# Attention and a routed feed-forward: routing choices in one pass, spaced key and value rows

## The chip, the cores and the metric

The kernel runs on one core of a Trainium2 chip. The metric is the time of one execution on the device in microseconds, lower is better. One execution was also taken by the hardware profiler; its rows are quoted below. TensorE appears as PE, its weight loads as PEld, VectorE as DVE, ScalarE as ACT, GpSimd as POOL and SyncE as SP.

## The reference

Masked attention over 8 batches of 8 heads, sequence 576 and head width 64, whose output is the input of a mixture of experts over 4608 tokens of width 512. Every token takes the best of 4 groups and in it the best of 4 experts, and its output is that expert's feed-forward (hidden width 1024) weighed by both softmax weights.

```python
mask_plain = (rel >= 0) & (rel < 32)
mask_dil = (rel >= 0) & (rel < 128) & (rel % 4 == 0)
# heads 0-3 plain, heads 4-7 dilated
scores = np.where(masks[None], scale * q @ k.T, -1e9)
attn = softmax(scores); x = (attn @ v) -> (4608, 512)
g_idx = np.argmax(x @ w_group, axis=1); g_w = softmax(...)[g_idx]
e_idx = np.argmax(x @ w_expert[g_idx], axis=1); e_w = softmax(...)[e_idx]
out = (g_w * e_w)[:, None] * (np.maximum(x @ w1[g, e], 0) @ w2[g, e])
```

## The kernel before

**Attention.** The batches are taken in four pairs (NBP), each in nine tiles (NJ) of 64 positions, 36 tiles (NT). One tile covers all 16 sequences of the pair. The loop `for s in range(NT + 3)` is pipelined by hand: step s issues scores of tile s, the transposition of the probabilities of tile s-1 (transpose_p), the product with the values of tile s-2 (av, into the accumulator o, of which there is one), its normalisation on VectorE, and the transposition of the normalised x of tile s-3 (transpose_x). On VectorE a tile has the row maximum mx, d = s - mx, the sums den, their reciprocal, and x = o * den. The orders of TensorE and VectorE are those of the code; the two queues are not sorted again. Since o has one buffer, the next av can begin only when x has read it.

**Loads.** q, k and v come in by groups of three tiles (192 positions), SP's queue issues all loads and stores in order. load_k fills every other partition of kb with a row of 8 * 224 numbers (7,168 bytes) per half; load_v fills vt with three blocks of 8 * 65 numbers per partition, in pieces of two and one (4,160 and 2,080 bytes a row, 6,240 where all three go at once). GpSimd makes a shifted copy of v (shift_v).

**Routing.** When the nine tiles of a pair are through, route(bp) follows, a Python generator that issues the routing of its 1152 tokens (TPB = 9 blocks of 128) in steps: the logits by TensorE (lt_ps, lg_ps), the choice of the group and then of the expert in it (top1, called twice), the one-hot matrix E, the ranks of the tokens within their expert by matmuls (rk_ps), the slot of each token, its split in a high part and 7 low bits (hl), the gate gt (written to the token's row in DRAM), and two masks, ohl (which of 128 low values) and mv (which high value, times the token's number). Their product tb_ps over nine blocks of tokens is the table of tokens by slot (tab). `yield` ends a step; a step that ends in `yield 2` closes the gate until the next av has been issued. slot() is called five times per tile, between VectorE's five instructions of attention, and runs fine[0] steps of the routing in hand. pick(r) chooses the expert with most tokens so far, for an early FFN, after the routings of two and of three pairs. The routings of the first three pairs run beside attention, the fourth in the tail.

**Tail.** After the last tile a string, TAIL, says in which order the rest is issued: R a part of the last route up to a gate, a and b a step of the first and second early FFN, w a chunk of weights. A chunk is split into two 16-bit parts: wb1h and the like on ScalarE, the rest wb1l on VectorE, which needs the first. After that come the 16 experts' FFNs, three matmuls per product (high times high, high times low, low times high).

Of the kernel before, what the change touches and what calls it, by code (L numbers as in the profile page):

```python
# [17 lines left out]
P = 128  # L18
# [27 lines left out]
TAIL = "aRaRaRawawwawRaRbwaRwbbwbbbwbwbw"  # L46
# [9 lines left out]
def moe_attention_kernel(ctx, tc, q, k, k0, v, cmask, wgate, wpack, out):  # L56
# [34 lines left out]
    KW = 8 * 224 + 96  # L91
# [67 lines left out]
    nc.gpsimd.iota(low, pattern=[[1, P]], base=0, channel_multiplier=0, allow_small_or_imprecise_dtypes=True)  # L159
    iota = low[:, 0:MAXOV]  # L160
# [19 lines left out]
    mine1 = cp.tile([P, TPB], F32, name="mine1")  # L180
# [4 lines left out]
    high = cp.tile([P, NE, NK4], F32, name="high")  # L185
# [29 lines left out]
    routes, gate, fine = [], [], [SLOTS]  # L215
# [7 lines left out]
    def scores(n):  # L223
# [144 lines left out]
    def route(bp):  # L368
# [24 lines left out]

        def top1(l4, nm):
            mx = T("mx" + nm, [TPB])
            nc.vector.tensor_reduce(mx, l4, axis=AX.X, op=ALU.max)
            yield 0
            mb = mx.unsqueeze(2).broadcast_to([P, TPB, 4])
            oh = T("oh" + nm, [TPB, 4])
            nc.vector.tensor_tensor(oh, l4, mb, ALU.is_equal)  # L400
            yield 0
            nc.vector.tensor_tensor(oh, oh, pri.unsqueeze(1).broadcast_to([P, TPB, 4]), ALU.mult)
            yield 0
            pm = T("pm" + nm, [TPB])
            nc.vector.tensor_reduce(pm, oh, axis=AX.X, op=ALU.max)
            yield 0
            nc.vector.tensor_tensor(oh, oh, pm.unsqueeze(2).broadcast_to([P, TPB, 4]), ALU.is_equal)
            df = T("df" + nm, [TPB, 4])
            nc.vector.tensor_tensor(df, l4, mb, ALU.subtract)
            yield 0  # L410
            return oh, df

        def total(df, nm):
            s = T("sm" + nm, [TPB])
            nc.vector.tensor_reduce(s, df, axis=AX.X, op=ALU.add)
            yield 0
            nc.vector.tensor_scalar_add(s, s, 1e-9)
            return s

        ohg, dfg = yield from top1(lg[:, :, 0:4], "g")  # L420
        yield 1
        pr = T("pr", [TPB, 4, 4])
        nc.vector.tensor_tensor(
            pr,
            lg[:, :, 4:20].rearrange("p t (g e) -> p t g e", g=4),
            ohg.unsqueeze(3).broadcast_to([P, TPB, 4, 4]),
            ALU.mult,
        )
        yield 0
        el = T("el", [TPB, 4])  # L430
        nc.vector.tensor_reduce(el, pr.rearrange("p t g e -> p t e g"), axis=AX.X, op=ALU.add)
        yield 0
        ohe, dfe = yield from top1(el, "e")
        E = E16[bp % 2]
        nc.vector.tensor_tensor(
            E[:, 0:TPB],
            ohg.unsqueeze(3).broadcast_to([P, TPB, 4, 4]),
            ohe.unsqueeze(2).broadcast_to([P, TPB, 4, 4]),
            ALU.mult,
        )  # L440
        yield 2
# [11 lines left out]
        for df in (dfg, dfe):  # L453
            nc.scalar.activation(df, df, AF.Exp, scale=1.0 / SX)
# [4 lines left out]
        nc.vector.tensor_copy(base[bp + 1], rk[:, TPB, :])  # L459
        nc.vector.tensor_tensor(rk[:, 0:TPB], rk[:, 0:TPB], Ef[:, 0:TPB], ALU.mult)  # L460
        yield 0
        mine = slice(bp * TPB, bp * TPB + TPB)
        nc.vector.tensor_reduce(slots[:, mine], rk[:, 0:TPB], axis=AX.X, op=ALU.add)
        yield 0
        sli = T("sli", [2, TPB], I32)
        nc.vector.tensor_copy(sli[:, 0], slots[:, mine])
        nc.vector.tensor_single_scalar(sli[:, 1], sli[:, 0], 7, ALU.arith_shift_right)
        yield 0
        hl = T("hl", [2, TPB])
        nc.vector.tensor_copy(hl[:, 1], sli[:, 1])  # L470
        nc.vector.scalar_tensor_tensor(hl[:, 0], hl[:, 1], -float(P), slots[:, mine], ALU.mult, ALU.add)
        yield 0
        sg = yield from total(dfg, "g")
        se = yield from total(dfe, "e")
        yield 0
        nc.vector.tensor_tensor(sg, sg, se, ALU.mult)
# [3 lines left out]
        own = xd[bp * TPB * P : (bp + 1) * TPB * P, DM:XW]  # L480
        nc.sync.dma_start(own.rearrange("(t p) o -> p t o", p=P), gt)
        tb_ps = psR.tile([P, NE * NK4], F32, name="tb_ps", tag="r")
        done = []
        for t0 in range(0, TPB, 3):
            ohl = sm.tile([P, 3, P], F16, name="ohl", bufs=2)
            nc.vector.tensor_tensor(
                ohl,
                low.unsqueeze(1).broadcast_to([P, 3, P]),
                hl[:, 0, t0 : t0 + 3].unsqueeze(2).broadcast_to([P, 3, P]),
                ALU.is_equal,  # L490
            )
            yield 0
            mv = sm.tile([P, 3, NE * NK4], F16, name="mv", bufs=2)
            for t in range(3):
                nc.vector.tensor_scalar(
                    mv[:, t],
                    high.rearrange("p e k -> p (e k)"),
# [672 lines left out]
```

## Time and profile before

| what | value |
|---|---|
| time, median of 3 runs | 610.18 us (608.88 to 617.73) |
| the profiled execution | 610.33 us |
| its span in the trace | 608.4 us |
| TensorE busy | 549.1 us, 90% |
| VectorE busy | 395.0 us, 65% |
| ScalarE, GpSimd busy | 316.8 and 206.1 us |
| instruction fetches | 63 of 1.03 MB in all (queue q8) |

The span is the time from the first to the last record of the trace; the profiled execution's own time holds 1.9 us more around it. Three stretches are told apart by their place in the program: attention with three routings up to about 185 us, the tail up to about 212 us, and the experts after that. A wait is the idle time of an engine ahead of an instruction, with what released it. "issue" means that nothing in the trace ended the wait. The granted clock is a share of TensorE's full speed.

### The profile page before, as it was taken

The page shows a single profiled execution, that of the slowest core. Times are in us where ns is not written, and L with a number is a line of the kernel's source. Part 1 is how long each engine was busy: PE and PEld are TensorE (multiplying, and loading weights), DVE is VectorE, ACT ScalarE, POOL GpSimd, SP SyncE. Part 2 cuts the span into 40 slices and gives each one's busy share as a digit, 9 for nine tenths or more (in the row PEclk, how much of TensorE's full clock was granted, in tenths as well). Part 3 has the DMA queues.
Part 4 walks back from the last instruction along what each step waited for, and adds up shares of the span by engine and source line. Part 5 has one row for each costly group of instructions (what it writes and reads, how often), then busy time and mean ns, then how long its engine had stood idle before and what let it go on. Part 6 is the DMA issues. An engine that isn't in the chain of part 4 may idle for free. (4 is left out here: it accounts for less than half of the span.)

```text
span 608.4 us, 18962 instructions
## 1 busy us (share of the span) xinstructions
PE 549.1 (90%) x7796; PEld 387.0 (64%) x7796; DVE 395.0 (65%) x923; ACT 316.8 (52%) x558; POOL 206.1 (34%) x243
## 2 busy tenths in 40 slices
PE   4787978879868599999999999999999999999985
PEld 2565756657556366656665666756657657787773
DVE  4465696796996772285577759767376577567730
ACT  3454434544564242374454647556486567566641
POOL 5886454544202022532033161322623502221211
PEclk9999989999989599999999999999999999999988
DMA  8988679777757416286959788696877989898840
GB/s 321 363 256 275 185 215 281 212 221 242 235 154 231 142 48 208 61 224 214 257 172 297 208 252 219 204 305 201 270 180 264 300 236 298 284 307 238 242 118 29
DMA packets 82764, 136.44 MB, mean 224 GB/s; under 512 B 43149, under 2 KB 52791, under 8 KB 82675
## 3 DMA queue, kind: packets, MB, share of 16 engines
q1 hardware_dynamic: 75746, 115.62, 63.4%
q0 software_dynamic: 6784, 19.51, 10.3%
q8 instruction: 63, 1.03, 0.7%
q14 instruction: 27, 0.21, 0.1%
q10 hardware_dynamic: 144, 0.07, 0.0%
HBM read 108.12 MB, written 19.29 MB: 209 GB/s over the span
## 5 line engine op out<-in xcount | busy, mean ns | idle before, releaser
L696 DVE SCALAR_TENSOR_TENSOR hl<-a,hh 128x256 f16<-128x256 f32 (+13 forms) x144 | 60.3, 423 | 83.5 <-ACT hh L695 67.8
L752 POOL DMA_INDIRECT out<-yr,sent x31 | 38.4, 1240 | 216.5 <-ACT yr L751 194.1
L688 PE MATMUL a<-xs,wb1h 128*128 128x256 f16 (+7 forms) x576 | 99.8, 279 | 0.9 <-ACT xs L664 0.5
L688 PE MATMUL a<-xs,wa1h 128*128 128x304 f16 (+7 forms) x576 | 96.3, 274 | 1.4 <-SPq L1081 0.9
L695 ACT ACTIVATE hh<-a 128x256 f16<-128x256 f32 (+13 forms) x144 | 55.7, 389 | 71.0 <-PE a L688 57.4
L781 PEld LDWEIGHTS <-hh 128*128 128x128 f16 x480 | 46.9, 98 | 54.6 <-issue 1.2
L688 PE MATMUL a<-xs,wb1l 128*128 128x256 f16 (+7 forms) x288 | 79.3, 279 | 0.6 <-DVE wb1l L603 0.6
L688 PE MATMUL a<-xs,wa1l 128*128 128x304 f16 (+7 forms) x288 | 77.5, 274 | 0.1
L688 PEld LDWEIGHTS <-wb1h 128*128 128x128 f16 x576 | 55.9, 99 | 13.3 <-issue 0.6
L688 PEld LDWEIGHTS <-wa1h 128*128 128x128 f16 x576 | 55.2, 99 | 13.0 <-issue 2.0
L631 POOL DMA_INDIRECT xr<-xd,sent x41 | 42.1, 1027 | 45.4 <-DVE key L560 23.1
L117 POOL TENSOR_SCALAR vs<-vt 32x520 f32<-32x520 f32 (+1 forms) x48 | 41.1, 856 | 46.0 <-DMA vt<-v 38.4
L603 DVE SCALAR_TENSOR_TENSOR wa2l<-w,wa2h 128x1024 f16<-128x1024 f32 x32 | 38.6, 1219 | 26.7 <-ACT wa2h L606 24.5
L603 DVE SCALAR_TENSOR_TENSOR wb2l<-w,wb2h 128x1024 f16<-128x1024 f32 x32 | 38.8, 1222 | 21.4 <-ACT wb2h L606 19.2
L279 PE MATMUL o<-vs,pt 64*32 64x65 f32 x1152 | 34.1, 232 | 17.8 <-DVE x L335 12.3
L781 PE MATMUL y<-wa2h,hh 128*128 128x512 f16 x120 | 45.6, 380 | 0.5 <-issue 0.5
L781 PE MATMUL y<-wb2h,hl 128*128 128x512 f16 x120 | 45.5, 379 | 0.5 <-DVE hl L696 0.5
L781 PE MATMUL y<-wb2h,hh 128*128 128x512 f16 x120 | 45.6, 380 | 0.0
L781 PE MATMUL y<-wb2l,hh 128*128 128x512 f16 x120 | 45.5, 379 | 0.0
L781 PE MATMUL y<-wa2l,hh 128*128 128x512 f16 x120 | 45.5, 379 | 0.0
L781 PE MATMUL y<-wa2h,hl 128*128 128x512 f16 x120 | 45.5, 379 | 0.0
L253 DVE TENSOR_REDUCE mx<-s 128x8 f32<-128x512 f32 x36 | 24.7, 687 | 30.8 <-PE s L243 30.8
(199 smaller groups left out, 1210.5 us busy)
## 6 DMA issues: line engine op xcount, KB each, us to landing
w<-wpack SPq DMA_DIRECT2D x128, 512.0 KB
kb<-k SPq DMA_DIRECT2D x24, 448.0 KB
qb<-q SPq DMA_DIRECT2D x28, 256.0 KB
vt<-v SPq DMA_DIRECT2D x11, 520.0 KB
xd<-x SPq DMA_DIRECT2D x24, 192.0 KB
vt<-v SPq DMA_DIRECT2D x11, 260.0 KB
qb<-q SPq DMA_DIRECT2D x2, 768.0 KB
xd<-x SPq DMA_DIRECT2D x32, 48.0 KB
```

The costliest lines, as they stand in the source:

```text
L117: nc.gpsimd.tensor_scalar(vs[g][even, j0:j1], vt[g][even, j0:j1], 1.0, 1.0, ALU.mult, ALU.mult)
L253: nc.vector.tensor_reduce(mx, s, axis=AX.X, op=ALU.max)
L279: nc.tensor.matmul(o[32 * j : 32 * j + 32, w, c * 65 : c * 65 + 65], pt[n % NPT][64 * w : 64 * w + 64, c, 32 * j : 32 * j + 32], (vs, vt)[ ...
L603: nc.vector.scalar_tensor_tensor(l, w32, SW, h, ALU.mult, ALU.subtract)
L631: nc.gpsimd.indirect_dma_start(out=xr[0:n], out_offset=None, in_=xd[0:known, :], in_offset=bass.IndirectOffsetOnAxis(ap=ent[0:n, t : t + 1 ...
L688: nc.tensor.matmul(a[:, 0:cap], ww[:, c * FF + f * P : c * FF + f * P + P], xx[:, c, 0:cap], start=(i == 0), stop=(i == len(mm) - 1),)
L695: nc.scalar.activation(hh[:, f, 0:cap], a[:, 0:cap], AF.Relu)
L696: nc.vector.scalar_tensor_tensor(hl[:, f, 0:cap], a[:, 0:cap], 0.0, hh[:, f, 0:cap], ALU.max, ALU.subtract)
L752: ins = nc.gpsimd.indirect_dma_start(out=out, out_offset=bass.IndirectOffsetOnAxis(ap=ent[0:n, t : t + 1], axis=0), in_=yr[0:n, :], in_off ...
L781: nc.tensor.matmul(yp, h[:, f, t * P : t * P + n], ww[:, f * DM : f * DM + DM], start=(i == 0), stop=(i == len(mm) - 1),)
```

## The change

It has three parts. **Routing:** the maxima, one-hots and differences of the group and of all four groups' experts are taken at once, over 5 * 9 rows of four, and E is one product of both; exponential on 180 elements. The sums, the gate's reciprocal (now on 9 elements) and the update of base follow after the product tb_ps, and the gate is spread to 16 columns by ScalarE. The masks mv are two instructions over 128x576 in 16 bit, ohl three of 128x384 with a 16-bit index row; the nine tb_ps matmuls stand together after one gate. fine[0], the number of steps per slot, is 1 until the third routing starts and 2 (SLOTS) from there on; it was 2 throughout. **Loads:** the four parts of a k row lie 456 numbers apart in kb and the three blocks of a v row 528 numbers apart in vt, so that one row is moved in pieces of 1,792 or 2,080 bytes. **Tail:** the string is another.

```diff
-TAIL = "aRaRaRawawwawRaRbwaRwbbwbbbwbwbw"
+TAIL = "aRaRawawawRwawbwabRwabbwbbbwbw"
-    KW = 8 * 224 + 96
+    KC = 448 + 8
+    KW = 4 * KC + 96
         for w in halves:
-            nc.sync.dma_start(kb[g % NK][w:P:2, w, 0 : 8 * 224], k[g, w])
+            nc.sync.dma_start(
+                kb[g % NK][w:P:2, w, 0 : 4 * KC].rearrange("p (c n) -> p c n", n=KC)[:, :, 0:448],
+                k[g, w].rearrange("p (c n) -> p c n", n=448),
+            )
-            vt[g] = vp.tile([P, 3, 8, 65], F32, name="vt")
+            vt[g] = vp.tile([P, 3, 528], F32, name="vt")[:, :, 0:520].rearrange("p j (s c) -> p j s c", c=65)
-    high = cp.tile([P, NE, NK4], F32, name="high")
+    high = cp.tile([P, NE, NK4], F16, name="high")
-    routes, gate, fine = [], [], [SLOTS]
+    routes, gate, fine = [], [], [1]
-                    c0 = sl * w + 32 * (jl + a)
+                    c0 = sl * w + 32 * (jl + a) + (8 * (sl // 2) if n else 0)
...
-        ohg, dfg = yield from top1(lg[:, :, 0:4], "g")
-        yield 1
...
-        ohe, dfe = yield from top1(el, "e")
+        n5 = 5 * TPB
+        l5 = lg.rearrange("p t (g e) -> p (t g) e", e=4)
+        mx = T("mx5", [n5])
+        nc.vector.tensor_reduce(mx, l5, axis=AX.X, op=ALU.max)
+        yield 0
+        mb = mx.unsqueeze(2).broadcast_to([P, n5, 4])
+        oh = T("oh5", [n5, 4])
+        nc.vector.tensor_tensor(oh, l5, mb, ALU.is_equal)
...
+        ohv = oh.rearrange("p (t g) e -> p t g e", g=5)
+        ohg = ohv[:, :, 0, :]
         E = E16[bp % 2]
         nc.vector.tensor_tensor(
-            E[:, 0:TPB],
-            ohg.unsqueeze(3).broadcast_to([P, TPB, 4, 4]),
-            ohe.unsqueeze(2).broadcast_to([P, TPB, 4, 4]),
-            ALU.mult,
+            E[:, 0:TPB], ohg.unsqueeze(3).broadcast_to([P, TPB, 4, 4]), ohv[:, :, 1:5, :], ALU.mult
         )
...
-        gt = T("gt", [TPB, XW - DM])
-        nc.vector.reciprocal(gt, sg.unsqueeze(2).broadcast_to([P, TPB, XW - DM]))
...
+        mv = T("mv", [TPB, NE * NK4], F16)
+        nc.vector.tensor_tensor(
+            mv,
+            high.rearrange("p e k -> p (e k)").unsqueeze(1).broadcast_to([P, TPB, NE * NK4]),
+            hl[:, 1].unsqueeze(2).broadcast_to([P, TPB, NE * NK4]),
+            ALU.is_equal,
+        )
+        yield 0
+        nc.vector.tensor_tensor(mv, mv, mine1.unsqueeze(2).broadcast_to([P, TPB, NE * NK4]), ALU.mult)
+        yield 0
+        ohl = T("ohl", [TPB, P], F16)
         for t0 in range(0, TPB, 3):
-            ohl = sm.tile([P, 3, P], F16, name="ohl", bufs=2)
...
-            for t in range(3):
-                nc.vector.tensor_scalar(
-                    mv[:, t],
...
+        yield 2
+        tb_ps = psR.tile([P, NE * NK4], F32, name="tb_ps", tag="r")
+        for t in range(TPB):
+            nc.tensor.matmul(tb_ps, ohl[:, t], mv[:, t], start=(t == 0), stop=(t == TPB - 1))
+        s5 = T("s5", [n5])
+        nc.vector.tensor_reduce(s5, df, axis=AX.X, op=ALU.add)
...
+        nc.vector.reciprocal(sg, sg)
+        gt = T("gt", [TPB, XW - DM])
+        nc.scalar.copy(gt, sg.unsqueeze(2).broadcast_to([P, TPB, XW - DM]))
...
+        nc.vector.tensor_copy(base[bp + 1], rk[:, TPB, :])
         yield 1
...
-            if n == NBP - 3:
+            if n == NBP - 2:
                 fine[0] = SLOTS
```

VectorE's row before, in the tile of the first routing that makes the masks: mx, d, den, the reciprocal of den and x are attention's, all else is the routing's.

```order
L255 TENSOR_TENSOR d<-s,mx 128x512
L417 TENSOR_SCALAR sme<-sme 128x9
L476 TENSOR_TENSOR smg<-smg,sme 128x9
L328 TENSOR_SCALAR den<-o 128x8
L479 RECIPROCAL gt<-smg 128x144
L486 TENSOR_TENSOR ohl<-low,hl 128x384
L495 TENSOR_SCALAR mv<-high,hl,mine_204 128x64 x3
L330 RECIPROCAL den<-den 128x8
L486 TENSOR_TENSOR ohl<-low,hl 128x384
L495 TENSOR_SCALAR mv<-high,hl,mine_204 128x64 x3
L335 TENSOR_TENSOR x<-o,den 128x2x4x64
L253 TENSOR_REDUCE mx<-s 128x8
```

VectorE's row in the changed kernel, in the tile of the first routing that makes the masks (high and low_174 are index rows, hl the split slots).

```order
L259 TENSOR_REDUCE mx<-s 128x8
L457 TENSOR_TENSOR mv<-high,hl 128x576
L261 TENSOR_TENSOR d<-s,mx 128x512
L464 TENSOR_TENSOR mv<-mv,mine_206 128x576
L334 TENSOR_SCALAR den<-o 128x8
L468 TENSOR_TENSOR ohl<-low_174,hl 128x384
L336 RECIPROCAL den<-den 128x8
L468 TENSOR_TENSOR ohl<-low_174,hl 128x384
L341 TENSOR_TENSOR x<-o,den 128x2x4x64
L468 TENSOR_TENSOR ohl<-low_174,hl 128x384
L259 TENSOR_REDUCE mx<-s 128x8
```

Between den and x there stand two ohl in place of gt, two ohl and six mv; the masks mv are made between mx and den, and the gate's sums have left this place.

VectorE's row before, in the tail, from the early FFN's hl to the split of the last routing's slots; wb1l are the low halves of the second early expert's weights.

```order
L696 SCALAR_TENSOR_TENSOR hl<-a,hh 128x128 x2
L603 SCALAR_TENSOR_TENSOR wb1l<-w_3925,wb1h 128x1024
L603 SCALAR_TENSOR_TENSOR wb1l<-w_3927,wb1h 128x1024
L457 TENSOR_TENSOR rk<-rk_ps,base_150 128x160
L459 COPY base_151<-rk 128x16
L460 TENSOR_TENSOR rk<-rk,E_199 128x144
L463 TENSOR_REDUCE slots<-rk 128x9
L466 CAST sli<-slots 128x9
L467 TENSOR_SCALAR sli<-sli 128x9
L470 CAST hl<-sli 128x9
L471 SCALAR_TENSOR_TENSOR hl<-hl,slots 128x9
```

VectorE's row in the changed kernel at the same place of the tail.

```order
L686 SCALAR_TENSOR_TENSOR hl<-a,hh 128x128 x3
L593 SCALAR_TENSOR_TENSOR wb1l<-w_3829,wb1h 128x1024
L438 TENSOR_TENSOR rk<-rk_ps,base_150 128x160
L441 TENSOR_TENSOR rks<-rk,E_201 128x144
L444 TENSOR_REDUCE slots<-rks 128x9
L447 CAST sli<-slots 128x9
L449 TENSOR_SCALAR sli<-sli 128x9
L452 CAST hl<-sli 128x9
L454 SCALAR_TENSOR_TENSOR hl<-hl,slots 128x9
L457 TENSOR_TENSOR mv<-high,hl 128x576
L464 TENSOR_TENSOR mv<-mv,mine_206 128x576
L468 TENSOR_TENSOR ohl<-low_174,hl 128x384 x3
L593 SCALAR_TENSOR_TENSOR wb1l<-w_3831,wb1h 128x1024
L593 SCALAR_TENSOR_TENSOR wb1l<-w_3833,wb1h 128x1024
```

One split of weights stands ahead of rk where there were two, no gate sum follows the split of the slots, and two more splits come after the masks.

ScalarE's row before, in the tail, at the high halves wb1h of the second early expert's weights; xs is the second early FFN's input, yr an output of the first.

```order
L606 ACTIVATE wb1h<-w_3925 128x1024
L606 ACTIVATE wb1h<-w_3927 128x1024
L606 ACTIVATE wb1h<-w_3929 128x1024
L454 ACTIVATE dfg<-dfg 128x36
L454 ACTIVATE dfe<-dfe 128x36
L751 ACTIVATE yr<-y,cse_223 128x512
L664 CAST xs<-pt 128x4x128 x2
L606 ACTIVATE wb1h<-w_3931 128x1024
L606 ACTIVATE wb2h<-w_3950 128x1024
```

ScalarE's row in the changed kernel at the same place.

```order
L596 ACTIVATE wb1h<-w_3829 128x1024
L685 ACTIVATE hh<-a 128x128
L596 ACTIVATE wb1h<-w_3831 128x1024
L435 ACTIVATE df_3812<-df_3812 128x180
L596 ACTIVATE wb1h<-w_3833 128x1024
L596 ACTIVATE wb1h<-w_3835 128x1024
L654 CAST xs<-pt 128x4x128 x2
L596 ACTIVATE wb2h<-w_3869 128x1024
```

The fourth wb1h stands ahead of the casts of xs, and no yr stands ahead of them.

## Rows read from the trace of the kernel before

**Rows 1.** Windows: stretch, its length, busy us (instructions) by engine, clock, DMA share, GB/s.

```profile
0.00:60.00 60.00, 42.42 (x1150) 30.63 (x1151) 31.02 (x97) 26.57 (x48) 41.90 (x71) 0.96 0.87 303
60.00:185.00 125.00, 102.40 (x3021) 79.21 (x3023) 101.62 (x295) 62.91 (x137) 49.74 (x69) 0.96 0.73 216
212.00:608.00 396.00, 385.84 (x3457) 264.70 (x3455) 242.38 (x472) 217.66 (x356) 111.11 (x102) 0.99 0.74 217
```

**Rows 2.** Waits of TensorE, 60 to 185 us: us in total, times, longest.

```profile
PE o L279 <- DVE x L335: 12.3, 7, 3.6
PE o L279 <- issue: 3.2, 5, 1.1
...
PE o L279 <- DVE sli L466: 0.4, 1, 0.4
```

**Rows 3.** Waits of TensorE in the first 60 us.

```profile
PE o L279 <- issue: 6.8, 4, 2.4
```

**Rows 4.** Timeline of VectorE, first routing's masks: start, us, instruction, [idle before].

```profile
81.53 1.05 DVE L479 RECIPROCAL gt<-smg 128x144 f32<-128x144 f32 x1
82.50 0.49 DVE L486 TENSOR_TENSOR ohl<-low,hl 128x384 f16<-128x384 f32 x1
...
84.11 1.37 DVE L495 TENSOR_SCALAR mv<-high,hl,mine 128x64 f16<-128x64 f32 x3
85.39 0.68 DVE L335 TENSOR_TENSOR x<-o,den 128x512 f32<-128x512 f32 x1
```

**Rows 5.** Windows at half clock: two after waits in attention, one in the tail.

```profile
86.28:89.70 3.42, 3.42 (x87) 2.59 (x91) 3.26 (x7) 1.54 (x3) 3.03 (x4) 0.50 0.60 123
171.62:175.03 3.41, 3.41 (x81) 3.01 (x68) 3.38 (x9) 1.17 (x3) 0.00 (x0) 0.50 0.56 118
198.93:212.58 13.65, 8.34 (x40) 5.68 (x41) 10.64 (x33) 3.46 (x5) 1.02 (x1) 0.50 0.44 131
```

**Rows 6.** Timeline of TensorE in the tail: tb_ps and the FFN's first low half.

```profile
202.23 0.23 PE L510 MATMUL tb_ps<-mv,ohl 128*128 128x64 f16 x1 [6.04 <-DVE mv L495]
...
210.10 0.40 PE L688 MATMUL a<-xs,wb1l 128*128 128x256 f16 x1 [0.63 <-DVE wb1l L603]
```

**Rows 7.** Timeline of VectorE in the tail.

```profile
195.32 2.51 DVE L603 SCALAR_TENSOR_TENSOR wb1l<-w,wb1h 128x1024 f16<-128x1024 f32 x2 [3.07 <-ACT wb1h L606]
197.75 0.32 DVE L457 TENSOR_TENSOR rk<-rk_ps,base 128x160 f32<-128x160 f32 x1
...
204.14 0.75 DVE L495 TENSOR_SCALAR mv<-high,hl,mine 128x64 f16<-128x64 f32 x3
...
208.83 1.22 DVE L603 SCALAR_TENSOR_TENSOR wb1l<-w,wb1h 128x1024 f16<-128x1024 f32 x1
```

**Rows 8.** Timeline of ScalarE in the tail.

```profile
205.01 0.59 ACT L664 CAST xs<-pt 128x512 f16<-128x512 f32 x1 [6.35 <-issue]
...
206.30 1.06 ACT L606 ACTIVATE wb1h<-w 128x1024 f16<-128x1024 f32 x1
```

**Rows 9.** The page's DMA issues: transfer, queue, times, KB each.

```profile
kb<-k SPq DMA_DIRECT2D x24, 448.0 KB
...
vt<-v SPq DMA_DIRECT2D x11, 520.0 KB
...
vt<-v SPq DMA_DIRECT2D x11, 260.0 KB
```

**Rows 10.** Timeline of TensorE: two waits that no engine ends.

```profile
26.97 0.21 PE L279 MATMUL o<-vt,pt 64*32 64x65 f32 x1 [2.20 <-issue]
...
42.55 0.38 PE L243 MATMUL s<-kb,qb 128*32 128x128 f32 x2 [0.98 <-issue]
```

**Rows 11.** DMA queues, 21.2 to 24.7 us: packets, MB, share of 16 engines.

```profile
q1 hardware_dynamic: 416, 1.38, 101.4%
```

**Rows 12.** DMA queues, 24.7 to 25.8 us.

```profile
q8 instruction: 1, 0.02, 5.2%
```

**Rows 13.** DMA queues, 42.6 to 44.5 us.

```profile
q1 hardware_dynamic: 410, 0.54, 81.8%
```

More of the change, by code (lines that the diff above doesn't have):

```diff
@@ L159, in moe_attention_kernel @@
     nc.gpsimd.iota(low, pattern=[[1, P]], base=0, channel_multiplier=0, allow_small_or_imprecise_dtypes=True)
+    low16 = cp.tile([P, P], F16, name="low16")
+    nc.gpsimd.iota(low16, pattern=[[1, P]], base=0, channel_multiplier=0, allow_small_or_imprecise_dtypes=True)
     iota = low[:, 0:MAXOV]
@@ L179, in moe_attention_kernel @@
     )
-    mine1 = cp.tile([P, TPB], F32, name="mine1")
+    mine1 = cp.tile([P, TPB], F16, name="mine1")
     nc.gpsimd.iota(
@@ L452, in route @@
             )
-        for df in (dfg, dfe):
-            nc.scalar.activation(df, df, AF.Exp, scale=1.0 / SX)
+        nc.scalar.activation(df, df, AF.Exp, scale=1.0 / SX)
         yield 0
@@ L458, in route @@
         yield 0
-        nc.vector.tensor_copy(base[bp + 1], rk[:, TPB, :])
-        nc.vector.tensor_tensor(rk[:, 0:TPB], rk[:, 0:TPB], Ef[:, 0:TPB], ALU.mult)
+        rks = T("rks", [TPB, NE])
+        nc.vector.tensor_tensor(rks, rk[:, 0:TPB], Ef[:, 0:TPB], ALU.mult)
         yield 0
         mine = slice(bp * TPB, bp * TPB + TPB)
-        nc.vector.tensor_reduce(slots[:, mine], rk[:, 0:TPB], axis=AX.X, op=ALU.add)
+        nc.vector.tensor_reduce(slots[:, mine], rks, axis=AX.X, op=ALU.add)
         yield 0
@@ L507, in route @@
-            yield 2
-            for t1, lo, hv in done:
-                for t in range(3):
-                    nc.tensor.matmul(tb_ps, lo[:, t], hv[:, t], start=(t1 + t == 0), stop=(t1 + t == TPB - 1))
-            done.clear()
+            if t0 < TPB - 3:
+                yield 0
+        yield 2
[3 more added lines that the diff above has]
+        s5 = T("s5", [n5])
@@ new lines, in route @@
+        nc.vector.tensor_reduce(s5, df, axis=AX.X, op=ALU.add)
+        yield 0
+        nc.vector.tensor_scalar_add(s5, s5, 1e-9)
+        yield 0
+        es = T("es", [TPB, 4])
+        s5v = s5.rearrange("p (t g) -> p t g", g=5)
+        nc.vector.tensor_tensor(es, s5v[:, :, 1:5], ohg, ALU.mult)
+        yield 0
+        sg = T("sg", [TPB])
+        nc.vector.tensor_reduce(sg, es, axis=AX.X, op=ALU.add)
+        yield 0
+        nc.vector.tensor_tensor(sg, sg, s5v[:, :, 0], ALU.mult)
+        yield 0
@@ new lines, in route @@
+        nc.vector.reciprocal(sg, sg)
+        gt = T("gt", [TPB, XW - DM])
+        nc.scalar.copy(gt, sg.unsqueeze(2).broadcast_to([P, TPB, XW - DM]))
+        own = xd[bp * TPB * P : (bp + 1) * TPB * P, DM:XW]
+        nc.sync.dma_start(own.rearrange("(t p) o -> p t o", p=P), gt)
+        yield 0
+        add = T("add", [NE * NK4])
+        nc.vector.tensor_scalar(add, tb_ps, 0.5, float(bp * TPB * P - 1 - NTOK), ALU.is_gt, ALU.mult)
+        yield 0
+        nc.vector.tensor_tensor(add, add, tb_ps, ALU.add)
@@ L512, in route @@
         yield 0
         tf = tab.rearrange("p e k -> p (e k)")
-        add = T("add", [NE * NK4])
-        nc.vector.tensor_scalar(add, tb_ps, 0.5, float(bp * TPB * P - 1 - NTOK), ALU.is_gt, ALU.mult)
-        nc.vector.tensor_tensor(add, add, tb_ps, ALU.add)
         nc.vector.tensor_tensor(tf, tf, add, ALU.add)
+        nc.vector.tensor_copy(base[bp + 1], rk[:, TPB, :])
         yield 1
```

65 lines of the change are left out of this document (11 added, 54 removed).

## The prediction

> **What bounds the kernel now.** I read the busy time by stretches first [rows 1]. From 212 us to the end TensorE is busy for 385.84 of 396 us at a granted clock of 0.99: nothing that the change touches can be gained there, beyond what starts that part earlier. Before that TensorE is idle for 17.58 us of the first 60 and 22.60 us of the next 125, and from 60 to 185 us VectorE is about as busy as TensorE, 101.62 against 102.40 us. So the waits of TensorE come next. From 60 to 185 us [rows 2] the largest is the product of probabilities and values, o, waiting for VectorE's x of the tile before: 12.3 us in 7 waits, the longest 3.6. Another 6.2 us in seven smaller lines wait for VectorE or, through it, for ScalarE's exponential of d, so 18.5 us in all. 3.2 us are waits of o that no engine ends ("issue"), and in the first 60 us that kind takes 6.8 us in 4 waits [rows 3]. A timeline of VectorE under the largest wait, next, shows why x is late [rows 4]: between den and x of one tile stand the gate reciprocal (1.05 us), two ohl (0.49 the first), and two groups of three mv (the second 1.37). x starts at 85.39 and o follows at 86.22. [...]
>
> The tail (185 to 212 us) is the last routing with an early expert's FFN beside it. TensorE's tb_ps product waits there 6.04 us for mv, and the FFN's first low half waits for wb1l until 210.10 us [rows 6]. On VectorE [rows 7] two wb1l splits run from 195.32, rk starts at 197.75, the last three mv end at 204.89 and the fourth wb1l runs from 208.83 to 210.05. ScalarE's fourth wb1h starts only at 206.30, behind two casts of xs of which the first begins at 205.01 [rows 8].
>
> **A. The routing beside attention.** A routing has the same matmuls as before. On VectorE it loses the 144-wide reciprocal (1.05), nine mv and some of the small steps, and gains two mv of 128x576. The trace has no such shape. Below lies the ohl with 384 elements at 0.49, above it 576/512 of x's 0.68 [rows 4], thus 0.5 to 0.8 us each; I take 0.75, the nearer size. Three mv take 0.75 in the tail [rows 7] and 1.37 here, so nine cost 2.25 to 4.1 us, and 0.7 to 2.6 us go there. With the reciprocal, some 2 to 3.5 us of VectorE per routing, 6 to 10 us in the three that lie beside attention. That would still be hidden work if it did not stand between den and x. There it did: from gt's start at 81.53 to x's at 85.39, 3.9 us. In the new order this place holds two ohl, about 1.0 us, so the delay of x falls by about 3 us in the worst tile, nearly the whole of the 3.6 us wait. All other tiles of the first two routings hold one small step per slot in place of two; the price is that each routing is spread over about eight tiles. Five short steps per tile lie in slots where VectorE had idle time waiting for s, except in the third routing, which still runs two steps per slot with three ohl between den and x.
> Of the 18.5 us I leave 7.5: one tile of the third routing at about 2 us, the exponential's waits, and small ones in the eight tiles of each routing. That gives 11 us. Not all comes back: the issue waits below stand beside the VectorE waits, and a TensorE that runs ahead of VectorE meets its next instructions sooner. At 10.0 us of issue waits over 185 us, of which the tiles without routing have their share, I take back 4. **A is −7 us**, from 0 (all eaten) to −14 (three quarters of 18.5).
>
> **B. The clock.** The stretches at 86.28 and 171.62 us hold 3.4 us of TensorE work each at half clock; at full clock each would take 1.7. They follow waits that A removes. I take one of them gone, **−1.5 us**, from 0 to −3.4.
>
> **C. The tail.** One split instead of two stands ahead of rk on VectorE: 2.51/2 = 1.25 us earlier. The chain from rk to the last mask was 197.75 to 204.89, 7.1 us; without five gate sums and the base copy (six small steps at about 0.18, an estimate from rk's 0.32 on more elements), without the reciprocal (1.05), and with two mv at 0.75 for 2.25, it is about 4.2. Casts of xs no longer wait behind tb_ps, and the fourth wb1h stands ahead of them, so ScalarE has it by about 200 us and not at 207.36. Then only VectorE's own row sets the fourth wb1l: its start at 208.83 less the reciprocal (1.05), the mv (0.75), those six small steps and three more of add and tab, now later (nine at 0.18), 3.4 us, so it ends near 206.7. **C is −3 us**, with −5 if the clock comes up earlier too and −0.5 if xs or the weights' loads are late instead. In the tail there is still a wait before tb_ps, so I leave the half clock there. The early expert's choice comes one or two tiles later in the new order; its weights' loads are in SP's queue behind the same stores, and have at least 20 us before the tail, so I cost that at nothing; if they came late, C goes to its upper end.
>
> **D. The packets.** 24 loads of k at 448 KB and the loads of v [rows 9] now go in pieces of 1,792 and 2,080 bytes in place of 7,168 and 4,160 or 6,240. What these have to do with TensorE: the wait of 2.20 us at 26.97 us has no engine behind it [rows 10]. Over the 3.5 us from 21.2 us the load queue took the 16 DMA engines for 101.4% with 416 packets of 3.3 KB on average and no instruction fetch got in [rows 11]; right after, from 24.7 to 25.8 us, one instruction fetch of 0.02 MB lands [rows 12], and TensorE goes on at 26.97. The wait of 0.98 us at 42.55 us stands next to a stretch with 410 packets of 1.3 KB [rows 13]. So the stall is shorter where packets are smaller, by two cases. If the four issue waits of the first 60 us (6.8) and five later ones (3.2) all fell as 2.20 to 0.98, 5.5 us would go; removed wholly, with those that A brings out, 9. Only part of the queue is k and v; stores of x and loads of q keep their packets. I take −1.5. Against it stands the price of small packets: 16 engines × 3.5 us × 101.4% over 1.38 MB is 41 us of engine time per MB, and the same from rows 13 (16 × 1.9 × 81.8% over 0.54) is 46. For about 20.6 MB of k and v (24 × 448 KB, 11 × 520 KB, 11 × 260 KB and the first) that is at most 5 × 20.6 / 16 = 6.4 us of DMA, hidden as long as the share, 0.87 in the first 60 us and 0.73 after [rows 1], has room. **D is −1.5 us**, from +2 to −9.
>
> [...]
>
> **The sum** is −7 −1.5 −3 −1.5 = −13 us against the profiled execution of 610.33 us (its span of 608.4 and 1.9 around it): 597 us. The median of the runs, 610.18, is the same to 0.15 us.
>
> **Rivals.** 1. The instruction stream sets the tile's pace: TensorE's waits for x turn into issue waits, A shrinks to −1 and B to 0, and packets bring nothing, with C at −3 and some small waits left: about 605 us. For it: issue waits are as long as 2.20 us, and at 0 to 60 us, where VectorE is not the limit, they are the largest kind. Against: from 60 to 185 us they are 3.2 us beside 18.5. [...] 2. The packets remove most issue waits, D is −9 and A needs nothing back: with A at −10, B −1.5 and C −3 some 23 us, 588 us. For it: rows 11 and 12, the fetch landing only as the queue lets go. Against: only two cases, and a stretch of one size can stall or not. 3. Slower: the smaller packets make DMA the pace of attention. Where the share reaches 1 for long, k and v come late, the gains of A and B are waits for loads instead, and all of the 6.4 us shows; with C, 610.3 + 6.4 − 3 = 614 us. It decides once the share from 60 to 185 us, 0.73, comes near 1; that it is 0.87 in the first 60 us speaks for it, that 6.4 us over 185 is 0.03 of share speaks against. 4. The order does not do what it says: if x is as late as before, since five steps per tile cost more than the idle time that takes them in, A is nothing; that is the upper end of A and lies with rival 1.
>
> **How the numbers follow.** Forecast 0.52 at 597 us, with 591 to 603 as its own range; rivals 1 and 4 0.24 at 605; rival 2 0.16 at 588; rival 3 0.08 at 614. For 8 in 10, leaving out rival 3 and the outer parts of rivals 1 and 2: 586 to 608. 2% is about what a measurement of this kernel tells from no change; 2% faster is below 598.0. Of the forecast somewhat more than half lies there, 0.30, and all of rival 2: 0.46; over 622.4 is the far end of rival 3: 0.03; the rest, 0.51, is within 2%.
>
> **What the profile after would show.** A: the line of o waiting for x from 60 to 185 us falls from 12.3 to under 5 us; if "issue" has taken its place, rival 1. B: the windows after those waits have a clock of 1. C: the first low-half matmul of the early FFN starts about 3 us sooner after the last attention tile. D: the issue waits of the first 60 us fall below 5 us, at a DMA share of 0.87 to 0.9. The forecast is wrong if the third routing, two steps per slot, costs as much as the first two saved, or if the tail waits for weights.

## The result and the profile after

The changed kernel takes 601.12 us (median of 20 runs, 595.81 to 607.36) where the kernel before takes 610.25 in the same comparison; the ratio of the two is 0.9854 (95% interval 0.9825 to 0.9884), 8.9 us less. I had forecast 597, with 586 to 608 as the range: the sign and the range held, the gain is two thirds of the 13 us of the sum. The profiled execution took 603.41 us, 2.3 above the median (its span 601.5). Here and below the times are medians of all executions, while the ratios leave out executions over 1.5% longer than the fastest of their kernel, so that a ratio need not be the quotient of the two medians.

The windows of the changed kernel answer to [rows 1] (same columns).

```profile
0.00:60.00 60.00, 43.05 (x1234) 31.21 (x1234) 33.50 (x101) 28.89 (x50) 39.37 (x69) 1.00 0.88 290
60.00:185.00 125.00, 103.39 (x2998) 79.81 (x2999) 92.22 (x247) 65.05 (x136) 55.83 (x73) 0.97 0.77 224
212.00:601.00 389.00, 378.32 (x3412) 258.49 (x3410) 239.77 (x467) 214.60 (x350) 107.13 (x102) 1.00 0.76 220
```

From 60 to 185 us VectorE is busy for 92.22 us where it was 101.62, and TensorE for a microsecond more than before. The last stretch is the experts' part, which starts earlier and is shorter by what came before it alone. The last transposition of x ends at 180.69 us where it ended at 183.31, and the first output of the first full expert begins at 255.23 where it was 261.76. TensorE's timeline at these two places, first before, then after:

```profile
182.68 0.63 PE L356 MATMUL tx<-id,x 128*128 128x128 f32 x4 [1.15 <-DVE x L335]
...
261.76 0.39 PE L781 MATMUL y<-wa2h,hh 128*128 128x512 f16 x1
...
180.06 0.63 PE L362 MATMUL tx<-id,x 128*128 128x128 f32 x4 [1.09 <-DVE kk L534]
...
255.23 0.39 PE L771 MATMUL y<-wa2h,hh 128*128 128x512 f16 x1
```

Of 6.5 us in these two profiled executions 2.6 come before the tail and 3.9 in it.

The waits of TensorE from 60 to 185 us, for [rows 2] (us in total, times, longest):

```profile
PE o L285 <- issue: 7.7, 6, 2.9
PE o L285 <- DVE x L341: 4.3, 5, 2.3
PE lt_ps L387 <- issue: 3.0, 2, 2.1
PE tx L362 <- ACT d L267: 1.9, 1, 1.9
```

and in the first 60 us, for [rows 3]:

```profile
PE o L285 <- issue: 5.2, 4, 2.7
...
PE s L249 <- DMA kb<-k: 1.2, 1, 1.2
```

The wait of o for x has fallen from 12.3 us to 4.3 in this trace, under the 5 that were forecast. The waits of o without a releaser have risen from 3.2 to 7.7 us, and the logits (lt_ps) now have 3.0 us of that kind too; the first 60 us give 5.2 for 6.8, where the prediction asked for less than 5. So part of what VectorE no longer holds up is now held up by something else, the first alternative that the prediction named.

The timeline of VectorE in the tile that held TensorE up for 3.57 us before, for [rows 4]:

```profile
83.32 0.16 DVE L334 TENSOR_SCALAR den<-o 128x8 f32<-128x8 f32 x1
83.40 0.90 DVE L468 TENSOR_TENSOR ohl<-low,hl 128x384 f16<-128x384 f16 x1
84.22 0.19 DVE L336 RECIPROCAL den<-den 128x8 f32<-128x8 f32 x1
84.33 0.85 DVE L468 TENSOR_TENSOR ohl<-low,hl 128x384 f16<-128x384 f16 x1
85.11 0.68 DVE L341 TENSOR_TENSOR x<-o,den 128x512 f32<-128x512 f32 x1
```

Between den and x stand two ohl and the reciprocal, as the order said. They are not 0.5 us each, though, but 0.90 and 0.85; GpSimd's copies of v (vs) run beside them, from 81.61 to 85.66 us. x starts 1.79 us after den, where it was nearly 4. TensorE's o behind it, in its timeline:

```profile
85.93 0.21 PE L285 MATMUL o<-vs,pt 64*32 64x65 f32 x1 [0.76 <-DVE x L341]
```

0.76 us of wait are left of 3.57.

The granted clock fell to 0.50 in three stretches before the last expert, for [rows 5]; in the kernel before there were two more in attention, at 28.26 and 58.98 us, and those of the rows.

```profile
61.09:64.50 3.41, 3.41 (x43) 2.73 (x35) 0.00 (x0) 0.47 (x1) 3.11 (x5) 0.50 0.91 278
166.90:170.31 3.41, 3.13 (x81) 2.99 (x82) 3.31 (x10) 0.63 (x1) 0.00 (x0) 0.50 0.50 104
201.03:204.45 3.42, 2.65 (x18) 1.92 (x18) 1.84 (x4) 0.11 (x1) 0.29 (x1) 0.50 0.92 340
```

The stretch at 86 us has gone. The other one in attention that the prediction named, at 171.62 us, has not: it stands at 166.90, around a wait of 2.31 us of o for x that ends at 167.18. The stretch in the tail is 3.4 us long where it was 13.65.

The tail on VectorE, for [rows 7]:

```profile
192.33 1.22 DVE L593 SCALAR_TENSOR_TENSOR wb1l<-w,wb1h 128x1024 f16<-128x1024 f32 x1
193.46 0.32 DVE L438 TENSOR_TENSOR rk<-rk_ps,base 128x160 f32<-128x160 f32 x1
...
196.66 1.49 DVE L468 TENSOR_TENSOR ohl<-low,hl 128x384 f16<-128x384 f16 x3
198.07 2.35 DVE L593 SCALAR_TENSOR_TENSOR wb1l<-w,wb1h 128x1024 f16<-128x1024 f32 x2
...
201.06 0.68 DVE L655 TENSOR_TENSOR xs<-pt,xs 128x512 f16<-128x512 f32 x1
201.66 1.22 DVE L593 SCALAR_TENSOR_TENSOR wb1l<-w,wb1h 128x1024 f16<-128x1024 f32 x1
```

on TensorE, for [rows 6]:

```profile
198.45 0.27 PE L678 MATMUL a<-xs,wb1h 128*128 128x256 f16 x1 [2.75 <-ACT xs L654]
...
201.80 0.37 PE L678 MATMUL a<-xs,wb1h 128*128 128x256 f16 x1 [3.08 <-DVE xs L655]
...
204.10 0.26 PE L479 MATMUL tb_ps<-mv,ohl 128*128 128x64 f16 x1
```

and on ScalarE, for [rows 8]:

```profile
190.87 1.06 ACT L596 ACTIVATE wb1h<-w 128x1024 f16<-128x1024 f32 x1 [3.91 <-DMA w<-wpack]
...
196.38 1.06 ACT L596 ACTIVATE wb1h<-w 128x1024 f16<-128x1024 f32 x1 [0.22 <-DMA w<-wpack]
197.34 0.57 ACT L654 CAST xs<-pt 128x512 f16<-128x512 f32 x1
```

rk starts behind one split at 193.46 and the masks end at 198.15, 4.7 us later where it took 7.1. The fourth wb1l ends at 202.88, 22.2 us after the last transposition of x, where it was 26.7 us (210.05 after 183.31). tb_ps no longer waits. What waits now is the second early FFN for xs (2.75 and 3.08 us), whose row on VectorE stands behind two splits, and an early FFN for hl. TensorE's waits for tb_ps in the tail before, and for hl after:

```profile
PE tb_ps L510 <- DVE mv L495: 6.5, 2, 6.0
...
PE a L678 <- DVE hl L686: 3.2, 2, 1.8
```

The matmul at 210.10 us in [rows 6] is not the first low half of the second early FFN but its fourth, and the fourth wb1l held it up for 0.63 us only. The first low half, before and after, starts without a wait:

```profile
207.35 0.42 PE L688 MATMUL a<-xs,wb1l 128*128 128x256 f16 x1
...
201.96 0.42 PE L678 MATMUL a<-xs,wb1l 128*128 128x256 f16 x1
```

That is 24.0 us after the last transposition of x, then 21.3: 2.8 us sooner, as the prediction asked.

### The profile page after: what moved, and what is told of

It reads as the page before. It is cut to its first block, busy times and chain, and to the rows that moved or that the text cites. A ratio compares the mean times of both kernels' runs of the same rounds, so it can differ in the third digit from the quotient of the medians.

```text
span 601.5 us, 18903 instructions
## 1 busy us (share of the span) xinstructions
PE 542.7 (90%) x7796; PEld 382.7 (64%) x7796; DVE 384.7 (64%) x863; ACT 320.7 (53%) x558; POOL 204.0 (34%) x244
## 3 DMA queue, kind: packets, MB, share of 16 engines
q0 software_dynamic: 6784, 19.51, 10.3%
## 5 line engine op out<-in xcount | busy, mean ns | idle before, releaser
L742 POOL DMA_INDIRECT out<-yr,sent x31 | 35.3, 1140 | 215.4 <-ACT yr L741 200.9
L678 PE MATMUL a<-xs,wa1l 128*128 128x304 f16 (+7 forms) x288 | 77.1, 272 | 0.4 <-DVE wa1l L593 0.4
L121 POOL TENSOR_SCALAR vs<-vt 32x520 f32<-32x520 f32 (+1 forms) x48 | 42.7, 889 | 43.1 <-DMA vt<-v 35.4
L741 ACT ACTIVATE yr<-y,cs 128x512 f32<-128x512 f32 (+3 forms) x31 | 21.3, 687 | 46.9 <-PE y L771 33.7
```

Source lines behind the costliest of these rows:

```text
L121: nc.gpsimd.tensor_scalar(vs[g][even, j0:j1], vt[g][even, j0:j1], 1.0, 1.0, ALU.mult, ALU.mult)
L678: nc.tensor.matmul(a[:, 0:cap], ww[:, c * FF + f * P : c * FF + f * P + P], xx[:, c, 0:cap], start=(i == 0), stop=(i == len(mm) - 1),)
L741: nc.scalar.activation(yr[0:n, :], yp[0:n, :], AF.Copy, scale=cs[0:n, t : t + 1])
L742: ins = nc.gpsimd.indirect_dma_start(out=out, out_offset=bass.IndirectOffsetOnAxis(ap=ent[0:n, t : t + 1], axis=0), in_=yr[0:n, :], in_off ...
```

## The experiments

Every ratio is against the kernel before on the same chip. Beside the times I read one number of each trace: when the last transposition of x ends, with what TensorE idled until then.

**Spaced rows alone.** The kernel before with this part of the change and no other.

```diff
-    KW = 8 * 224 + 96
+    KC = 448 + 8
+    KW = 4 * KC + 96
...
-            vt[g] = vp.tile([P, 3, 8, 65], F32, name="vt")
+            vt[g] = vp.tile([P, 3, 528], F32, name="vt")[:, :, 0:520].rearrange("p j (s c) -> p j s c", c=65)
...
-                    c0 = sl * w + 32 * (jl + a)
+                    c0 = sl * w + 32 * (jl + a) + (8 * (sl // 2) if n else 0)
```

> The kernel before with the spaced rows of k and v alone. Theory 1 (the packets do nothing to the waits of TensorE that no engine ends; the gain lies in the routing and the tail): 609 to 611 us, and the issue waits of o from 0 to 185 us stay at 9 to 12 us. Theory 2 (smaller packets shorten these waits, the extra ones of the changed kernel come from elsewhere): 604 to 607 us, issue waits of o at most 7 us. Theory 3 (smaller packets cost DMA time that the changed kernel hides in other gains): 612 to 615 us.

614.54 us by before's 614.21, ratio 1.001 (0.9968 to 1.0051). The issue waits of o in the first 60 us:

```profile
PE o L283 <- issue: 7.0, 4, 2.7
```

and from 60 to 185 us, with the wait for x above them:

```profile
PE o L283 <- DVE x L339: 11.8, 6, 3.3
PE o L283 <- issue: 7.1, 6, 2.9
```

Those two lines of issue waits make 14.1 us where the kernel before had 10.0. By themselves the packets shorten no wait here; the interval of the time (2.0 us faster to 3.1 slower) would still hold the forecast 1.5.

**The change without spaced rows**, taken twice: the four lines above back to the kernel before's, all else as changed.

> The changed kernel with k and v rows whole, as before. Theory 1 (packets do nothing): 600 to 602 us. Theory 2 (packets shorten the waits): 604 to 607 us, with issue waits of o from 0 to 185 us above 15 us. Theory 3 (packets cost): 596 to 599 us.

605.67 us, ratio 0.9899 (0.9861 to 0.9938). The issue waits of o up to the end of attention are 12.1 us, not the more than 15 that theory 2 wanted; the changed kernel has 12.8.

> The changed kernel with whole rows once more, beside the two halves of it. If the halves add up: its ratio is the product of theirs within 0.004. If packets do nothing: a ratio of 0.984 to 0.989 as the changed kernel has; if they bring 2 us or more there: 0.988 to 0.992.

605.6 us, ratio 0.9893 (0.9838 to 0.9948). The changed kernel has 0.9854 and 0.9855, so spaced rows may be worth 0.4% there, 2.4 us. No pair settles it; the two pairs put together give 0.43% with about 0.39% either way (an estimate from the four intervals), just clear of nothing. In the traces the gain isn't in attention, where the rows are loaded (below).

**The old tail string.**

```diff
-TAIL = "aRaRawawawRwawbwabRwabbwbbbwbw"
+TAIL = "aRaRaRawawwawRaRbwaRwbbwbbbwbwbw"
```

> The changed kernel with the tail string of before. If the tail's share of the gain (about 4 us between the last transposition of x and the first output of the first full expert) comes from the string: 604 to 606 us. If it comes from the shorter chain of choices on VectorE, whatever the string: 600 to 602 us.

607.15 us by 614.21, ratio 0.9865 (0.9785 to 0.9945), too wide to tell from the time. The trace tells: from the last transposition of x to the first output of the first full expert it takes 74.3 us, the changed kernel 74.5 and 74.7, the kernel before 78.5. No gain of the string is seen in this one trace; the new routing is what remains.

**Two steps per slot throughout.**

```diff
-    routes, gate, fine = [], [], [1]
+    routes, gate, fine = [], [], [SLOTS]
```

> The changed kernel with two routing steps per slot throughout, as before; three ohl then stand between den and x in the first two routings too. If the spread over more tiles is what brings attention's share: 603 to 606 us, and waits of o for x from 60 to 185 us of 8 us or more in place of 4.3. If the cheaper steps alone bring it: 600 to 602 us. If the spread only gave TensorE more of the waits that no engine ends: 597 to 600 us.

608.17 us by 614.21, ratio 0.9935 (0.9892 to 0.9977). Slower than the changed kernel, whose interval (0.9825 to 0.9884) ends below this one. But in the trace o waits for x for 4.8 us, hardly more than 4.3. The spread helps by the time (0.8%, 4.9 us, as much as the new routing beside attention brings in all, below), and not by the wait that I had named. Its one trace does not show where: attention ends at 182.33 us, between the 180.69 and 184.07 of two traces of the changed kernel.

**The changed kernel again**, for a second trace.

> The changed kernel once more, beside the next three. The same ratio as before, 0.982 to 0.989. Its second trace tells how much the waits that no engine ends differ from one execution to the next: if they are set by the program and the packets, 17 to 18 us in the first 181 us as in the first trace; if by chance, anything from 13 to 22.

602.15 us by 610.76, ratio 0.9855 (0.982 to 0.9891), and 17.7 us of issue waits in attention where the first trace has 17.5. The single waits stand elsewhere and o waits 7.0 us for x, not 4.3; attention ends at 184.07 us, 3.4 later than in the first trace. One trace of either kernel does not tell a difference of 3 us.

**No later loads.** q, k and v are loaded for the first groups alone.

```diff
     def load_q(g, j0=0, j1=3):
+        if g >= NQ:
+            return
...
-        for w in halves:
+        for w in halves if g < NK else ():
...
+        if g >= 3:
+            vt[g] = vt[g - 3]
+            return
```

> The changed kernel without the loads of q, k and v after the first three (k: two) groups: attention then computes on stale data, so its x and the routing that follows from it are others, and only attention is read, not the whole time. If TensorE's waits that no engine ends are instruction fetches behind the loads: they fall from 17 us to under 5 in the first 181 us, and the last transposition of x ends at 168 to 173 us in place of 181. If the fetches are slow by themselves, or the issue is not a fetch: 12 us or more remain, and it ends after 177.

Its whole time (1096.14 us) has no meaning here, since the routing of other data sends many tokens through the loop at the end. The waits of TensorE in the first 60 us, then from 60 us to the end of attention:

```profile
PE o L290 <- issue: 1.8, 3, 1.4
...
PE o L290 <- DVE x L346: 9.4, 6, 2.3
PE s L254 <- issue: 1.2, 1, 1.2
```

Nearly all issue waits have gone, 3.4 us are left of 17.5. The window of attention, ending with the last transposition of x, here and in the changed kernel:

```profile
0.00:167.34 167.34, 141.37 (x4129) 107.94 (x4130) 124.67 (x342) 90.25 (x181) 92.43 (x139) 0.95 0.48 129
...
0.00:180.69 180.69, 142.13 (x4130) 107.02 (x4130) 121.87 (x342) 91.53 (x181) 93.40 (x139) 0.98 0.81 249
```

It ends at 167.34 us, the DMA share is 0.48 where it is 0.81 until 180.69 us in the changed kernel. TensorE idles for 26.0 us of it where it is 38.6. The waits that no engine ends are thus caused by the loads, 14 us of them in the changed kernel. With them gone VectorE's x is the largest wait (9.4 us).

**Smaller rows of k**, eight pieces of 896 bytes.

```diff
-    KC = 448 + 8
-    KW = 4 * KC + 96
+    KC = 224 + 8
+    KW = 8 * KC + 96
...
-                    c0 = sl * w + 32 * (jl + a) + (8 * (sl // 2) if n else 0)
+                    c0 = sl * w + 32 * (jl + a) + (8 * sl if n else 0)
```

> The changed kernel with rows of k in eight pieces of 896 bytes in place of four of 1,792. Theory 1 (packet size does nothing to the waits, and the DMA share has room): 600 to 603 us by before's 610, ratio within 0.004 of the changed kernel's in this call. Theory 2 (smaller packets shorten the waits): faster by 2 to 4 us. Theory 3 (small packets cost): slower by 2 to 5 us, and TensorE waits for kb in attention.

602.65 us by 610.76, ratio 0.9865 (0.9824 to 0.9906): as the changed kernel. Its issue waits from 60 to 185 us:

```profile
PE s L249 <- issue: 4.8, 4, 2.0
...
PE o L285 <- issue: 4.1, 5, 1.8
```

With the rest they are 17.9 us in attention, as with pieces twice as long. From 7,168 to 896 bytes the size of the pieces does nothing to these waits that shows beside their spread from trace to trace (below), and its price does not show either.

**The chain first.** The changed kernel with the third R of the string ahead of the weight chunks, so that ranks and masks run while VectorE waits for the first wb1h.

```diff
-TAIL = "aRaRawawawRwawbwabRwabbwbbbwbw"
+TAIL = "aRaRaRawawawwawbwabRwabbwbbbwbw"
```

> The changed kernel with the tail's third R moved ahead of the weight chunks, so that VectorE does the last routing's ranks and masks in the 4.2 us in which it waits for the first wb1h. If the tail after the change is bounded by VectorE's row from that first wb1h on: 2 to 3 us faster than the changed kernel. If it is bounded by the landing of the weights: within 1 us of it. If TensorE waits longer for E in front of the first early FFN: slower by up to 1 us.

598.99 us by 610.76, ratio 0.982 (0.9779 to 0.986), where the changed kernel had 602.15 in the same comparison. The timeline of VectorE shows rk ahead of all splits:

```profile
182.33 0.32 DVE L438 TENSOR_TENSOR rk<-rk_ps,base 128x160 f32<-128x160 f32 x1 [0.21 <-PE rk_ps L428]
...
187.35 3.49 DVE L593 SCALAR_TENSOR_TENSOR wb1l<-w,wb1h 128x1024 f16<-128x1024 f32 x3
...
192.39 1.22 DVE L593 SCALAR_TENSOR_TENSOR wb1l<-w,wb1h 128x1024 f16<-128x1024 f32 x1
```

The fourth wb1l ends 19.1 us after the last transposition of x (193.61 after 174.47), 3.1 sooner than in the changed kernel, and the tail counted as above takes 70.6 us for 74.5, although TensorE now waits 2.0 us for E. It is the fastest kernel here; its interval and the changed kernel's overlap, though, and part of this trace is chance: it is of the shortest of six executions (593.01 us), and its attention, which the string does not touch, is the shortest of all kernels with all loads.

> The changed kernel with the third R ahead of the weight chunks and whole rows of k and v. If packets do nothing: the ratio of the chain first with spaced rows, 0.979 to 0.985. If they bring 2 us: 0.985 to 0.989.

With whole rows it takes 603.38 us by 614.96, ratio 0.986 (0.9804 to 0.9915), by its midpoint again 0.4% above the one with spaced rows, and again inside the interval. Here the fourth wb1l ends 21.9 us after the last transposition of x and the tail takes 74.9 us, where the two traces of the changed kernel with whole rows have 22.2 and 23.1, and 75.9 and 76.8: a gain of about 1.4 us in the tail, not 4.

**The tail alone and attention alone.** The kernel before with both routings in it: the new one for the fourth pair with the new string, or for the first three pairs with one step per slot for two.

```diff
-    lastr = [route(NBP - 1)]
+    lastr = [route_new(NBP - 1)]
```

> The kernel before with the new routing in the fourth routing alone, and the new tail string; no spaced rows, the first three routings as before. If the gain splits as the traces say (tail about 4 us, attention about 4 to 5, packets nothing): 606 to 607 us by before's 610.5, a ratio of 0.991 to 0.996. If the tail's gain is lost later or was chance in the traces: 0.997 to 1.002.

613.05 us by 614.96, ratio 0.9991 (0.9954 to 1.0027). In its trace the tail takes 75.3 us as counted above, against 78.5 and 77.1 with the routing of before. The time shows less of it than that, 0.6 us, but its interval reaches to 2.8. In this trace 2 us are lost again behind the tail: from the first output of the first full expert to the end of the span it takes 348.6 us, before and with spaced rows alone 346.7 and 346.5.

```diff
-            routes.append(route(n))
+            routes.append(route_new(n))
```

> The kernel before with the new routing in the first three routings alone, one step per slot for two of them; the fourth routing, the tail string and the rows of k and v as before. If the routing beside attention brings what my term A takes after give-back (7 us) with B (1.5): a ratio of 0.984 to 0.988. If the waits that no engine ends eat more of it, as the traces say: 0.990 to 0.995. If they eat all (rival 1): 0.997 to 1.001.

608.18 us by 614.96, ratio 0.9929 (0.9897 to 0.996), 4.4 us. The waits of TensorE from 60 to 185 us:

```profile
PE o L293 <- issue: 6.0, 6, 1.8
PE o L293 <- DVE x L349: 3.8, 2, 2.3
```

The product of the halves' ratios is 0.992, beside 0.9899 and 0.9893 for both without spaced rows: they add up within their intervals.

## Why the prediction was right in sign and too large

Since single traces differ by several microseconds I put together what the traces say of attention. Three have the routing of before in it (before, spaced rows alone, tail alone) and eight in the table the new one with one step per slot (the two of the changed kernel, smaller rows of k, chain first with either rows, the two without spaced rows, attention alone). All values are means in us, up to the end of the last transposition of x; waits are sums over the lines of the view of waits, by their releaser. A ninth trace with the new routing, that of the old tail string, is not in the table: it is of the second longest of that kernel's six executions (610.73 us), and has 185.3 for the end, 8.2 us of waits for VectorE or ScalarE and 22.3 of issue waits. With it the means of the new routing are 179.8, 10.6 and 17.3.

| | end | TensorE busy | idle | waits for VectorE or ScalarE | issue waits |
|---|---|---|---|---|---|
| routing of before, 3 traces | 186.9 | 145.8 | 41.1 | 17.2 | 14.6 |
| new routing, 8 traces | 179.1 | 142.6 | 36.5 | 10.9 | 16.7 |
| of these, spaced rows, 4 | 180.4 | 142.4 | 38.0 | 11.3 | 17.2 |
| of these, whole rows, 4 | 177.8 | 142.8 | 35.0 | 10.4 | 16.2 |

**A, the routing beside attention: the mechanism was right, the size was not.** The step that failed is "of the 18.5 us I leave 7.5", 11 us of gain before the give-back. The waits for VectorE and ScalarE fell by 6.4. The worst tile did what I had worked out (3.57 to 0.76 us), and VectorE's own work came out (9.4 us less up to that point, by the means, for my 6 to 10), but more waits remained than the 7.5. In the first trace of the changed kernel 7.8 us for VectorE and 3.5 for ScalarE are left, the pick of the early experts (1.1 and 0.8) among them, and one o behind x of 2.31 us at 167.18, which is the third routing's tile that I had put at about 2. And I priced from the trace of before with its 19.5 us, the highest of the three with that routing (17.4 and 14.8 in the others). The give-back I had put at 4 is 2 us in the means (issue waits 14.6 to 16.7), though 12.8 to 18.0 for the three of before make that soft. My 10.0 us of issue waits had counted those of o alone; all lines of that trace make 12.8. Net of both it is about −4 us for my −7, with the ninth trace too, and the run of attention alone, which also holds B, measures −4.4 us (−6.3 to −2.5) for my −8.5.

**B, the clock: the sign was right, the size small by half.** TensorE is busy for 3.2 us less with the same attention matmuls, which I put down to the half clock that is gone (13.6, 23.9 and 27.3 us of it up to that point in the three traces of before, 3.4 to 13.7 in the eight; mean granted clock 0.93 to 0.96, then 0.96 to 0.99). I had −1.5, with −3.4 as the end, priced from the trace with the least of it. Of the two stretches that I named one went; the other stays in all eight traces, where a stretch starts between 163 and 174 us. The rest moved with chance more than I had allowed for: they stand at other places in every trace (28.26 and 58.98 us before, 61.09 us in the changed kernel).

**C, the tail: the size came out in the traces, but not by the waits that I had priced.** −3 forecast; from the last transposition of x to the first full expert's output it takes 78.3 us with the last routing of before (78.5, 77.1, 79.4) and 75.6 with the new one and its string (seven traces, 74.5 to 76.8), −2.7. The chain of ranks and masks is shorter nearly as I had worked out (7.1 to 4.7 us, for my 4.2), and the wait of tb_ps for mv is gone. But my sum went by the end of the fourth wb1l, which held TensorE up for 0.63 us only, and the waits for xs and hl took the place of tb_ps. With the same 679 matmuls TensorE idles in the tail for 9.5 us with the last routing of before and for 9.0 with the new one: −0.5 us, which is what I had given for the case that xs is late. The other 2.2 us are shorter busy time (68.8 to 66.6 us). About 1.6 of them are the half clock of the tail, which I had left as it was: TensorE works at it for 7.8 us with the last routing of before and for 4.7 with the new one, and half of the difference is saved (an estimate from these means). Its stretches are 10.2 to 13.7 us long, then 3.4 to 10.2. So the step of C that failed is "I leave the half clock there", and it was luck that −3 came out. That one split stands ahead of rk in place of two is not shown to matter: with the old string the trace is as short. The tail alone measures −0.6 us (−2.8 at its end), so by the time C is not shown.

**D, the packets: the reasoning on their size was wrong.** I took two stalls beside two sizes of packet for a relation, and for the second I read the packets behind it: that wait ends at 42.55 us and [rows 13] begin at 42.6. From 36.7 to 40.2 us, up to the start of the fetch ahead of it, the queue of the kernel before shows

```profile
q1 hardware_dynamic: 399, 1.00, 85.3%
```

which is 2.5 KB per packet and not 1.3. In the changed kernel TensorE's timeline has this wait at 28 us:

```profile
28.45 0.21 PE L285 MATMUL o<-vt,pt 64*32 64x65 f32 x1 [2.74 <-issue]
```

with, in the 3 us before the fetch that precedes it, and then from 25.9 to 27.1 us, this on the queues:

```profile
q1 hardware_dynamic: 524, 0.92, 87.3%
...
q8 instruction: 1, 0.02, 5.7%
```

1.8 KB per packet where there were 3.3 [rows 11], and the stall is 2.74 us where it was 2.20 [rows 10]. The traces with spaced rows have 17.2 us of issue waits, those with whole rows 16.2 (12.6 to 18.9 from trace to trace), and pieces of 896 bytes give 17.9; in the first 60 us those of o stayed above the 5 us that I had named as the sign. Why the size of the pieces does not show in these waits, no run here tells. The other half of my reasoning held: that the waits come from the loads is shown, by the run without them (17.5 to 3.4 us). That a fetch is what is late, the traces show by its place, but closely: of 195 such waits before the end of attention in all fourteen traces 178 end 2.2 to 3.05 us after a fetch on q8 has started, while 15% of that time lies so behind a fetch. What may cost is the start: TensorE's waits for DMA take 9.1 us in attention with spaced rows and 7.9 with whole ones (means of five and of six traces).

What stays open is why the times favour spaced rows by 0.4% in the two pairs (changed kernel, chain first) although attention does not, so that D's −1.5 is not far from the time, without its reason. For the changed kernel the traces put it into the experts' part: from the first output of the first full expert to the end it takes 346.3 and 346.0 us with spaced rows and 348.6 and 350.4 with whole ones. But no k or v is loaded there, the chain first has 346.0 and 345.9, and spaced rows with the old string 348.9. TensorE idles in it for 2.8 to 5.3 us with the new routing and spaced rows and 4.0 to 8.1 with whole ones, and the one kernel with whole rows and the old routing throughout idles for 3.5. I have no cause for it, and it may be chance.

By the rivals: rival 1 (the instruction stream takes A) holds in its direction, at 2 us and not 6; rival 2 (its terms add up to 23.5 us and 587, not 588) and rival 3 fell with the packets, since the 896-byte pieces show no cost; rival 4 fell with x, which starts 1.79 us after den; the forecast case held, at its upper end (its own range was 591 to 603). In sum about −4 (A), −3 (B), −3 (C) and nothing clear (D) make −10 by the traces, where the times say −8.9.

## What to carry to other kernels

Waits of TensorE that no engine ends are to be tested by taking the loads away, not read from a single stall and the packets next to it: 14 us of attention here are the loads' doing, and no size of their pieces tried here changed it. Side work between two steps of a loop that hands one buffer back and forth delays the next step: here 2.2 us less between den and x took 2.8 us off the wait behind it. Move such work to slots behind the hand-over, and count the other waits that remain before the gain is written down. In a tail ahead of weights, put the chain that only needs what is already there before the work that waits for a transfer; here, moving one letter of the string took 4 and 1.4 us off the tail in two pairs of traces, while the times do not settle it. And when one wait of the engine is taken away, look for the next one before the whole wait is counted as gain: tb_ps no longer waits 6.5 us in the tail, and TensorE idles there for only 0.5 us less.

## What was not expected of the hardware

An ohl of 384 elements takes 0.50 us in the tail (1.49 for three), no less than with 32-bit inputs before (0.49), and 0.90 and 0.85 us in attention while GpSimd copies v; the third of that routing, at 85.71 us, takes 0.54 though a copy runs beside it too, so a copy alone does not decide it. Before, three mv took 0.75 without and 1.37 with it. Two executions of the same program, the changed kernel, differ by 3.4 us in attention alone, which is more than the 2.4 us that the spaced rows may be worth: TensorE is busy for 142.13 and 144.16 us of it (mean granted clock 0.98 and 0.96) and waits for VectorE for 7.8 and 10.3, while the issue waits are 17.5 and 17.7 us, at other places.
